# All roots by a product, a place of its own for the fourth weight piece, another word to look at, and finer stages with other dates, in a gated linear recurrence with a SwiGLU block behind it

## The chip, the cores and the metric

The kernel runs on one NeuronCore of one Trainium2 chip. The metric is the device time of one execution in microseconds (us), as a median of several runs. Beside it there is one execution taken by the hardware profiler; all durations of single instructions come from that one. Five engines work side by side, each through its own instructions in the order in which they were written: TensorE (PE, matrix products; its weight loads are listed apart as PEld), VectorE (DVE), ScalarE (ACT), GpSimd (POOL) and SyncE (SP), which here only issues transfers. ACT and POOL issue transfers too. An instruction that waits for another engine or a transfer holds up everything behind it on its own engine.

## The reference

Two blocks follow each other. The first is a recurrence over 768 steps for 4 batches of 8 heads with head size 48. The state of a head is a complex 48 x 48 matrix; its rows decay by a complex gate, and the output is the real part read by q:

```python
mag = np.sqrt(a_re * a_re + a_im * a_im)
scale = np.minimum(mag, 0.999) / (mag + 1e-06)
a_re_n, a_im_n = (a_re * scale, a_im * scale)
for t in range(S):
    new_re = ar * S_re - ai * S_im
    new_im = ar * S_im + ai * S_re
    kv = np.einsum('bhd,bhe->bhde', k[:, :, t], v[:, :, t])
    S_re, S_im = (new_re + kv, new_im)
    y[:, :, t] = np.einsum('bhd,bhde->bhe', q[:, :, t], S_re)
```

Its output, seen as 3072 tokens of 384 features, goes through a feed-forward block:

```python
rms = np.sqrt(np.mean(x * x, axis=-1, keepdims=True) + 1e-06)
xn = x / rms * rms_g
g = xn @ w_gate                        # 384 x 1536
silu = g * (1.0 / (1.0 + np.exp(-g)))
val = xn @ w_val
return (silu * val @ w_out).astype(np.float32)
```

All weights arrive as 64-bit floats, seen as pairs of 32-bit words, and are converted to float32 on the chip.

## The kernel before, in words

**Units and groups.** Each batch's 768 steps are cut into 6 chunks of 128, 24 chunks in all, numbered n. The gates are worked out for "units": chunks 0 and 1 alone, then two chunks at a time (`UNITS`). The feed-forward block takes two chunks at a time (`GROUPS`), 256 tokens.

**Gates** (`gates(u)`, stages "size", "root", "turn", "rot"). Scans over a chunk turn the gates into cumulated magnitudes and phases. ACT supplies squares, roots, arctangent and sines, for which it loads tables, DVE the scans and products. The result, k and q turned by their phase, lies in `rots`, and twelve SP transfers for each pair of chunks (six for each chunk) bring it into the layout by head, `kqs`. The last cumulated values, `ends`, go into `decays`.

**Chunks** (`attend(n)`, line 1135 on). PE computes the scores of k and q for 8 heads in 32-row blocks into banks 4 and 5; DVE copies them under the causal mask into `am` (COPY_PREDICATED). PE then sums `am` times v and q times the old state into bank 6 (`yT`). For the new state PE transposes k into banks 7 and 4, ACT copies it to `kt`, PE multiplies it by v, DVE adds the old state and scales it.

**Norm** (stage "norm"). ACT squares `yT`, PE sums the squares over features by a product with ones into a column of bank 7, DVE scales it into `ssv`, POOL raises it to the power -0.5 into `rs`, one number for each of 128 tokens, one to a partition. It has to be spread over all partitions along the free axis. For the chunks in `SENT` (4 to 21) POOL sends `rs` to a line of `sq` and from there to all partitions of `row`, two transfers one after the other. For the other six chunks PE multiplies `rs`, spread over 128 columns, by the identity into bank 7. DVE multiplies `yg` by the result into `xT`.

**Feed** (`feed(g, xT)`). Six times, PE forms two products of 512 columns (gate and value) in banks 0 to 3, ACT applies SiLU to the one, DVE multiplies the two into `hT`, whose first 3,072 words hold the hidden values of one group. The product with `w_out` follows: plain for groups 0 and 1, and from group 2 on by a scheme with seven instead of eight half-size products.

**Weights** (`narrow(i)`, `fetch`). Twelve pieces: six of 1,536 KB for `w_gate` and `w_val` in turn (512 columns each), then six of 768 KB for `w_out`. Each is brought by a POOL transfer to a place in `wo` or `hT` that is still free, ACT converts its low words in place, and three DVE instructions put the float32 together. After each transfer POOL copies one word of the piece into `junk`: the look that tells POOL that it has landed. Piece i + 2 is sent after the look at piece i. By `CLEAR` the fourth piece (i = 3) also waits until POOL has looked at the `kq` of chunk 1 (`cleared`, copies into `seen`).

**Order.** Nothing is executed as written. `Flow` records every operation with a planned duration, its engine, its data dependences by address range and, for some, a due time. It passes due times back from users to producers, adds a shift for the stage that an operation belongs to (`flow.shift`, keyed by stage name and number), and lays out the program by a list schedule: on each engine, of what is ready, the earliest due time goes first. The instructions are then issued in that order, so the table of shifts and the planned durations decide the order of every engine, SP's and POOL's included, without a change to what is computed. Until a planned time of 62 us, gaps planned for PE are filled with products on `rot` whose result nobody reads, meant as warming (`flow.warm`). All operations are issued at line 676, so the profile tells them apart by tiles.

The last two stores to `out` are issued on SP; then a word `bad` decides by a branch whether a general version runs, which it doesn't with these inputs.

Of the kernel before, what the change touches and what calls it, by code (L numbers as in the profile page):

```python
# [14 lines left out]
ALU = mybir.AluOpType  # L15
# [4 lines left out]
C = 128  # L20
# [441 lines left out]
class Flow:  # L462
# [9 lines left out]
    turn = 0.0  # L472
# [206 lines left out]
def fast(tc, ctx, qT, kT, v, a_re, a_im, w_gate, w_val, w_out, rms_g, out, H, bad):  # L679
# [231 lines left out]

    wwords = wo.rearrange("p c f -> p (c f)").bitcast(I32)
    hwords = hT.bitcast(I32)
    places = [wwords[:, 0:3072], wwords[:, 3072:6144], hwords[:, 3072:6144]] * 2
    raw = wwords[:, 4608:6144]
    places += [raw, hwords[:, 3072:4608], hwords[:, 4608:6144]] * 2

    AHEAD = 2
    landed = {}

    CLEAR = {3: 1}

    def fetch(i, piece, raw, eng):
        to, ap, c, f = piece
        rows, n = to.shape[1:]
        src = ap.bitcast(I32).rearrange("(c p) f -> p c f", p=P)[:, c, 2 * f:2 * (f + n)]
        raw3 = raw.rearrange("p (c f) -> p c f", c=rows)
        if eng == "POOL" and i >= AHEAD:
            wait = [landed[i - AHEAD]]
        elif eng == "POOL":  # L930
            wait = [begun[0]]
        else:
            wait = []
        if eng == "POOL" and i in CLEAR:
            wait = wait + [cleared[CLEAR[i]]]
        dma(raw3, src, eng, after=wait)
        if eng == "POOL":
            landed[i] = copy(junk, raw[0:1, 0:1], eng="POOL")
        words = raw.rearrange("p (n two) -> p n two", two=2)
        return words[:, :, 0], words[:, :, 1]  # L940

# [37 lines left out]
    EARLY = {0: -100.0, 1: -98.0}  # L979
    SUMMED = ()  # L980
    LIGHT = (0, 1, 2)
    SENT = range(4, N - 2)
    SLOW = 2.0
    turn = {}
    moved = {}
# [58 lines left out]
    def gates(u):  # L1044
        ns = UNITS[u]
        nt = len(ns)
        T = nt * C
        t = loaded.pop(u) if u in loaded else load_kq(u, load_gates(u))
        flow.stage = "size", u
        re, im, q, k = (t[x] for x in ("re", "im", "q", "k"))  # L1050
        t1, t2, t3, t4, t5 = (t[f"t{i}"] for i in range(1, 6))
        act(t1, re, AF.Square)
        act(t2, im, AF.Square)
        if u in SUMMED:
            sums = []
            for i in range(nt):
                cs = slice(i * C, (i + 1) * C)
                ps = bank()[:, 0:ND * C].rearrange("p (j t) -> p j t", j=ND)
                mms([(ps, ident, x[:, :, cs], a == 0, a == 1) for a, x in enumerate((t1, t2))],
                    2 * mm_time(ND * C))  # L1060
                sums.append(ps)
                act(t2[:, :, cs], ps, AF.Abs_reciprocal_sqrt)
        else:
            tt(t1, t1, t2, ALU.add)
            act(t2, t1, AF.Abs_reciprocal_sqrt)
        act(t2, t2, AF.Square, scale=-EPS_MAG, bias=ones)
        act(t3, re, AF.Abs_reciprocal_sqrt, due=-200.0 if u == 0 else None)
        act(t3, t3, AF.Square, due=-200.0 if u == 0 else None)
        if u in SUMMED:
            for i in range(nt):  # L1070
                cs = slice(i * C, (i + 1) * C)
                ts(t1[:, :, cs], sums[i], CAP * CAP, None, ALU.min)
        else:
            ts(t1, t1, CAP * CAP, None, ALU.min)
        for j in range(ND):
            for i in range(nt):
                cs = slice(i * C, (i + 1) * C)
                scan(t4[:, j, cs], t2[:, j, cs], t1[:, j, cs], 1.0, ALU.mult, ALU.mult)

        tt(t["f"], t["in"], t3.unsqueeze(1).to_broadcast([P, 2, ND, T]))  # L1080
        stt(im, t5, 2.0, t3, ALU.subtract, rev=True)
        act(re, re, AF.Abs, bias=mid)
        act(re, re, AF.Relu, bias=width, accum=range_[:, u:u + 1])

        flow.stage = "root", u
        root = act(t2, t4, AF.Abs_reciprocal_sqrt)
        act(t1, t2, AF.Square)
        stt(t1, t1, -0.5, t4, ALU.mult)
        stt(t2, t1, 1.5, t2, ALU.add)
        tt(q, q, t4)  # L1090

        roots.append(root)
        yield
        flow.stage = "turn", u
        act(im, im, AF.Arctan, after=roots[-2:])
        last = turn.get(u - 1) if ns[0] % NCH else None
        for j in range(ND):
            scan(t3[:, j], im[:, j], zeros[:, 0:T], last[:, j] if last is not None else 0.0,
                 ALU.add, ALU.add)
        n = t5.bitcast(I32)  # L1100
        act(n, t3, AF.Copy, scale=0.5 / PI)
        stt(im, n, -2 * PI, t3, ALU.mult, ALU.add)
        turn[u] = im[:, :, T - 1:T]
        act(t5, im, AF.Abs)
        act(t3, im, AF.Sin)
        act(t5, t5, AF.Sin, scale=-1.0, bias=halfpi)

        for i, n_ in enumerate(ns):
            e = slice(i * C + C - 1, i * C + C)
            tt(ends[:, :, n_:n_ + 1], t4[:, :, e], t2[:, :, e])  # L1110
        flow.stage = "rot", u
        tt(t["f"], t["f"], t2.unsqueeze(1).to_broadcast([P, 2, ND, T]))
        for i, n_ in enumerate(ns):
            cs = slice(i * C, (i + 1) * C)
            for a, f in enumerate((t5, t3)):
                x = tt(rots[n_ % 2][:, a * ND:(a + 1) * ND].rearrange("p j (o t) -> p j o t", t=C), t["kq"][:, :, :, cs],
                   f[:, :, cs].unsqueeze(2).to_broadcast([P, ND, 2, C]))
                if not started:
                    started.append(x)
        for n_ in ns:  # L1120
            moved[n_] = [dma(kqs[n_ % 2][r:D2:2 * ND], rots[n_ % 2][:, r], "SP") for r in range(2 * ND)]
            if n_ < 2:
                cleared[n_] = copy(seen, kqs[n_ % 2][:, 0, 0:1], eng="POOL")
        send_decays(u)


# [8 lines left out]
    def attend(n):  # L1135
# [12 lines left out]
        for a in range(2):  # L1148
# [3 lines left out]
            for h in range(HH):  # L1152
# [7 lines left out]
            o = am[:, a * HH:(a + 1) * HH]  # L1160
            add("DVE", [(nc.vector.copy_predicated, (), dict(out=pairs(o), mask=mask, data=pairs(s)))],
                0.15 + 1.04e-3 * HH * C, [causal, s, o], [o])
        prev, new = states[(n + 1) % 2], states[n % 2]
        ps = banks[6]
        yT = ps[:, 0:DM].rearrange("p (j t) -> p j t", j=ND)
# [13 lines left out]
                lines[c].append((o, l_, r_, x == 0, x == len(todo) - 1))  # L1179
        order = [lines[c][i] for i in range(len(lines[0])) for c in range(4)]  # L1180
        mms(order, len(order) * mm_time(C) / 4 * 1.06, mode=BLK)
        if not last:
            kt = kts[0]
            for a in range(2):
# [26 lines left out]
        else:  # L1211
# [7 lines left out]
        sv = ssv[:, n:n + 1]  # L1219
        ts(sv, col, 1.0 / DM, EPS_RMS, ALU.mult, ALU.add)  # L1220
        add("POOL", [(nc.gpsimd.tensor_tensor, (), dict(out=rss[n % 2], in0=sv, in1=mhalf,
                                                        op=ALU.pow))], 0.9, [sv, mhalf], [rss[n % 2]])
        if n in SENT:
            line = sq[0:1, 1]
            dma(line, rss[n % 2], "POOL", slow=SLOW)
# [36 lines left out]
    def feed(g, xT):  # L1262
# [28 lines left out]

        def finish():
            for n, ot in zip(ns, ots):
                dma(out[n * C:(n + 1) * C, :], ot)

        if not split:
            for i in range(2):
# [65 lines left out]
    for in_, limit, op in ((ef, P_MIN, ALU.is_ge), (ef, 1.0, ALU.is_le), (range_, 0.0, ALU.is_le),  # L1363
# [15 lines left out]
    flow.warm = dict(after=started, until=WARM, call=[  # L1379
        (nc.tensor.matmul, (banks[3][:, 0:C],), dict(lhsT=filler[:, 0:C], rhs=filler[:, C:2 * C], start=True, stop=True))])  # L1380
    flow.shift = {
        ("attend", 1): 2.2, ("attend", 2): -6.5, ("attend", 4): -25.0, ("attend", 6): -11.5, ("attend", 8): 2.6,
        ("attend", 11): 1.7, ("attend", 12): 1.6, ("attend", 13): 0.9, ("attend", 14): -0.9, ("attend", 16): 1.1,
        ("attend", 17): -2.4, ("attend", 19): -1.4, ("attend", 21): -56.0, ("attend", 22): -0.5,
        ("attend", 23): -2.6, ("feed", 0): 4.7, ("feed", 1): 14.7, ("feed", 3): 31.9, ("feed", 5): 3.0,
        ("feed", 6): 13.5, ("feed", 7): 15.3, ("feed", 8): 7.1, ("feed", 9): 8.2, ("feed", 10): 4.3,
        ("feed", 11): -43.3, ("kq", 0): -8.1, ("kq", 1): 1.6, ("kq", 2): 6.6, ("kq", 3): 54.9, ("kq", 5): -58.9,
        ("kq", 6): 46.3, ("kq", 7): -13.7, ("kq", 9): -3.3, ("kq", 10): 1.9, ("load", 1): 13.9, ("load", 2): -1.6,
        ("load", 3): -5.7, ("load", 9): -5.0, ("norm", 0): -16.0, ("norm", 1): -5.4, ("norm", 2): 0.8,
        ("norm", 3): 2.0, ("norm", 4): -15.2, ("norm", 6): 0.7, ("norm", 9): 0.2, ("norm", 10): 7.3,  # L1390
        ("norm", 11): -1.1, ("norm", 15): -51.1, ("norm", 17): -2.9, ("norm", 19): -11.8, ("norm", 23): -12.0,
        ("root", 0): 1.3, ("root", 1): -4.6, ("root", 2): -43.1, ("root", 3): -3.6, ("root", 4): 0.7,
        ("root", 6): 33.4, ("root", 9): -29.6, ("rot", 0): -25.0, ("rot", 1): 9.8, ("rot", 2): 1.2,
        ("rot", 3): -49.4, ("rot", 5): 0.3, ("rot", 7): 60.9, ("rot", 10): -1.2, ("size", 0): 1.2,
        ("size", 2): -2.8, ("size", 5): 1.5, ("size", 10): -45.3, ("size", 12): -9.1, ("turn", 1): -22.1,
        ("turn", 3): -14.5, ("turn", 8): 38.2, ("turn", 10): 3.3, ("turn", 11): -25.6, ("turn", 12): -4.1,
        ("w", 0): -2.4, ("w", 1): 1.0, ("w", 2): 0.3, ("w", 5): -13.7, ("w", 6): 5.7, ("w", 8): -5.6,
        ("w", 10): 7.1, ("w", 11): 6.2,
    }
    flow.schedule()  # L1400
    with tc.manual_schedule():
# [51 lines left out]
```

## Time and profile before

| what | value |
|---|---|
| median of 5 runs | 727.22 us (723.2 to 730.3) |
| profiled execution, its own time | 726.08 us |
| its span in the trace | 724.4 us |
| PE busy | 683.9 us in 6,900 instructions |
| DVE busy | 475.8 us |
| ACT busy | 327.6 us, 82.1 of it 64 table loads |
| POOL busy | 63.1 us |
| products `ident,rs` | 12 instructions (2 a product), 3.1 us |
| transfers `sq<-rs`, `row<-sq` | 18 each; 2.1 and 3.9 us from issue to landing |
| warming products on `rot` | 82 instructions, 46 of them from 23.8 to 32.0 us |
| first scores of chunk 0 | 32.0 us |
| first product of feed 0 | 55.1 us |
| last product | ends at 717.7 us |

In a line of the profile, `bank<-xT,wg 128*128 128x256 f32` names the written and the read tiles (buffer numbers left out), the part of the array and the shape; a float32 product appears as two instructions. The number after the name is a count or the busy time; what follows an arrow in waits is whom the engine waited for. A stage table gives the busy time of each engine within a stretch of time. The "chain" is followed back from the last instruction through whatever released each step.

### The profile page before, as it was taken

To read this page: it belongs to the slowest core of one execution; us is meant where nothing else is said; L and a number is where in the kernel's file an instruction comes from. 1 tells how busy PE (TensorE), PEld (TensorE's weight loads), DVE (VectorE), ACT (ScalarE), POOL (GpSimd) and SP (SyncE) were. 2 spreads that over 40 slices of the span, in tenths; PEclk is the share of its full clock that TensorE was granted. 3 is DMA by queue.
4 is the path that set the end of the run, shared out by engine and by line. 5 is a ranking of instruction groups with operands and counts; after the bars stand their busy time and mean duration, and the time that the engine had idled before them with its cause. 6 is when DMAs were issued, how large, how long until landed. Compare 5 with 4: busy or idle time off the path is not lost.

```text
span 724.4 us, 16265 instructions
## 1 busy us (share of the span) xinstructions
PE 683.9 (94%) x6900; PEld 601.1 (83%) x6900; DVE 475.8 (66%) x756; ACT 327.6 (45%) x448; POOL 63.1 (9%) x106
## 2 busy tenths in 40 slices
PE   0769989999999999999999999999999999999996
PEld 0768767886889889889889889889889889989995
DVE  8889967987886878778667877778542443125131
ACT  8667547876683664657224753636410120010010
POOL 3141200010001101000011000110100000000000
PEclk9989999999999999999999999999999999999999
DMA  8596674435745463562464733652131231000000
GB/s 298 169 324 172 212 216 98 130 81 143 195 99 155 118 141 70 112 171 87 126 150 125 201 41 106 180 122 84 34 70 29 67 96 22 23 1 2 23 1 27
DMA packets 104001, 81.84 MB, mean 113 GB/s; under 512 B 41936, under 2 KB 94416, under 8 KB 103920
## 3 DMA queue, kind: packets, MB, share of 16 engines
q1 hardware_dynamic: 98704, 64.98, 32.7%
q0 software_dynamic: 4416, 15.35, 9.2%
q8 instruction: 56, 0.92, 0.5%
q10 hardware_dynamic: 800, 0.39, 0.2%
q14 instruction: 25, 0.20, 0.1%
HBM read 55.84 MB, written 4.72 MB: 84 GB/s over the span
## 4 chain that ended last, share of the span: by engine, by line
PE 86%; DVE 7%; DMA 2%; ACT 2%; issue 1%; SPq 1%; POOL 1%; DVEq 0%; ACTq 0%
PE bank L676 86%; DVE wv L676 1%; DVE wo L676 1%; DVE turns L676 1%; DMA decay<-ends 1%; DVE wg L676 1%; SPq L676 1%; DMA in<-in_a_re_dram 1%; DMA kq<-rot 1%; DVE t L676 1%; ACT t L676 1%; POOL rs L676 1%; DVE rot L676 1%; DVE hT L676 0%; DVE am L676 0%
## 5 line engine op out<-in xcount | busy, mean ns | idle before, releaser
L676 PE MATMUL bank<-xT,wg 128*128 128x256 f32 x864 | 202.0, 384 | 0.3 <-DVE xT L676 0.3
L676 PE MATMUL bank<-xT,wv 128*128 128x256 f32 x864 | 199.6, 382 | 1.2 <-DVE hT L676 1.2
L676 PEld LDWEIGHTS bank<-xT,wv 128*128 128x128 f32 x864 | 161.6, 190 | 23.9 <-DVE hT L676 1.6
L676 PEld LDWEIGHTS bank<-xT,wg 128*128 128x128 f32 x864 | 161.8, 191 | 23.2 <-issue 1.0
L676 PE MATMUL bank<-wo,hT 128*128 128x192 f32 (+1 forms) x576 | 118.6, 358 | 0.3 <-DVE hT L676 0.3
L676 DVE TENSOR_TENSOR hT<-bank,sg 128x512 f32<-128x512 f32 x72 | 49.6, 690 | 103.8 <-PE bank L676 96.7
L676 ACT ACTIVATE sg<-bank 128x512 f32<-128x512 f32 x72 | 43.0, 597 | 164.4 <-PE bank L676 158.1
L676 PEld LDWEIGHTS bank<-wo,hT 128*128 128x128 f32 x576 | 96.9, 191 | 12.5 <-issue 1.8
L676 ACT ACT_TABLE_LOAD x64 | 82.1, 1283 | 19.5 <-DVE rot L676 13.3
L676 POOL TENSOR_TENSOR rs<-ssv,mhalf 128x1 f32<-128x1 f32 x24 | 21.9, 914 | 488.6 <-DVE ssv L676 458.2
L676 DVE TENSOR_TENSOR rot<-kin,turns 128x768 f32<-128x768 f32 x48 | 44.1, 952 | 4.4 <-DMA kq<-rot 4.1
L676 PE MATMUL bank<-sums,hT 128*128 128x192 f32 x240 | 44.6, 328 | 0.0
L676 ACT ACTIVATE kt<-bank 128x384 f32<-128x384 f32 x40 | 19.5, 490 | 55.0 <-PE bank L676 52.9
L676 DVE COPY_PREDICATED am<-causal,bank 128x512 f32<-128x512 int32 x48 | 33.5, 724 | 14.6 <-PE bank L676 14.4
L676 ACT ACTIVATE turns<-in 128x768 f32<-128x768 f32 (+1 forms) x39 | 30.0, 789 | 24.6 <-DVE in L676 12.0
L676 PEld LDWEIGHTS bank<-kq 96*32 96x32 f32 x1536 | 30.1, 110 | 12.6 <-issue 7.8
L676 PEld LDWEIGHTS bank<-sums,hT 128*128 128x128 f32 x240 | 39.7, 190 | 0.5
L676 PE MATMUL bank<-kq 96*32 96x32 f32 (+3 forms) x1536 | 35.1, 235 | 4.4 <-issue 1.9
L676 DVE TENSOR_TENSOR hT<-hT 128x768 f32<-128x768 f32 x40 | 38.2, 955 | 0.8
L676 PE MATMUL bank<-am,ve 128*32 128x128 f32 x768 | 37.0, 275 | 0.0
L676 ACT ACTIVATE t<-t 128x768 f32<-128x768 f32 (+1 forms) x39 | 30.8, 789 | 8.8 <-DVE t L676 8.4
L676 PE MATMUL bank<-kq,state 96*32 96x128 f32 x640 | 32.2, 272 | 0.0
(123 smaller groups left out, 726.1 us busy)
## 6 DMA issues: line engine op xcount, KB each, us to landing
kq<-rot SPq DMA_DIRECT2D x144, 128.0 KB, 2.4
kin<-in_q_dram SPq DMA_DIRECT2D x24, 192.0 KB, 4.1
kin<-in_k_dram SPq DMA_DIRECT2D x24, 192.0 KB, 4.1
wo<-in_w_gate_dram SPq DMA_DIRECT2D x6, 768.0 KB, 4.6
out_dram<-ot SPq DMA_DIRECT2D x24, 192.0 KB, 2.3
wo<-in_w_val_dram SPq DMA_DIRECT2D x6, 768.0 KB, 4.6
wo<-in_w_out_dram SPq DMA_DIRECT2D x6, 768.0 KB, 5.0
in<-in_a_re_dram SPq DMA_DIRECT2D x11, 384.0 KB, 4.8
```

The costliest lines, as they stand in the source:

```text
L676: fn(*args, **kw)
```

## The change

- `SENT` is empty: all 24 chunks spread their root by the product.
- `places`: the fourth piece goes to the first half of `hT` instead of the first half of the `wo` room; the fifth and sixth go to the two halves of the `wo` room. The wait for chunk 1's `kq` (`CLEAR`) moves from the fourth to the fifth piece.
- The look reads word 1 of the landed piece, a high word, instead of word 0, a low word that ACT overwrites. It is recorded with the transfer as its only predecessor, and with a planned 0.8 us instead of 0.2.
- The planned duration of the root on POOL goes from 0.9 to 1.2 us, that of the copies into `seen` to 1.2.
- Stage "attend" is cut into "attend", "y" and "state", and the table of shifts is another one.
- The last group's first store (chunk 22) is issued by ACT instead of SP.

```diff
-    places = [wwords[:, 0:3072], wwords[:, 3072:6144], hwords[:, 3072:6144]] * 2
+    places = [wwords[:, 0:3072], wwords[:, 3072:6144], hwords[:, 3072:6144], hwords[:, 0:3072]]
+    places += places[0:2]
...
-    CLEAR = {3: 1}
+    CLEAR = {4: 1}
...
-        dma(raw3, src, eng, after=wait)
+        sent = dma(raw3, src, eng, after=wait)
         if eng == "POOL":
-            landed[i] = copy(junk, raw[0:1, 0:1], eng="POOL")
+            landed[i] = add("POOL", [(nc.gpsimd.tensor_copy, (), dict(out=junk, in_=raw[0:1, 1:2]))], 0.8,
+                            after=[sent])
...
-    SENT = range(4, N - 2)
+    SENT = ()
...
                 cleared[n_] = copy(seen, kqs[n_ % 2][:, 0, 0:1], eng="POOL")
+                cleared[n_]["dur"] = 1.2
...
+        flow.stage = "y", n
         prev, new = states[(n + 1) % 2], states[n % 2]
...
+        flow.stage = "state", n
         if not last:
...
         add("POOL", [(nc.gpsimd.tensor_tensor, (), dict(out=rss[n % 2], in0=sv, in1=mhalf,
-                                                        op=ALU.pow))], 0.9, [sv, mhalf], [rss[n % 2]])
+                                                        op=ALU.pow))], 1.2, [sv, mhalf], [rss[n % 2]])
...
-                dma(out[n * C:(n + 1) * C, :], ot)
+                dma(out[n * C:(n + 1) * C, :], ot, "ACT" if n == N - len(ns) else "SP")
...
     flow.shift = {
-        ("attend", 1): 2.2, ("attend", 2): -6.5, ("attend", 4): -25.0, ("attend", 6): -11.5, ("attend", 8): 2.6,
...
-        ("w", 10): 7.1, ("w", 11): 6.2,
+        ("attend", 0): 29.8, ("attend", 1): -5.3, ("attend", 2): 1.1, ("attend", 3): -21.9, ("attend", 4): -0.4,
...
+        ("kq", 0): 21.0, ("kq", 1): 37.2, ("kq", 2): 93.1,
...
+        ("state", 0): 50.2, ("state", 3): -27.9, ("state", 4): -29.1, ("state", 13): -15.1,
...
     }
```

More of the change, by code (lines that the diff above doesn't have):

```diff
@@ L1381, in fast @@
     flow.shift = {
-        ("attend", 1): 2.2, ("attend", 2): -6.5, ("attend", 4): -25.0, ("attend", 6): -11.5, ("attend", 8): 2.6,
[L1383 to L1396, printed above, removed]
@@ L1397, in fast @@
-        ("w", 0): -2.4, ("w", 1): 1.0, ("w", 2): 0.3, ("w", 5): -13.7, ("w", 6): 5.7, ("w", 8): -5.6,
-        ("w", 10): 7.1, ("w", 11): 6.2,
+        ("attend", 0): 29.8, ("attend", 1): -5.3, ("attend", 2): 1.1, ("attend", 3): -21.9, ("attend", 4): -0.4,
+        ("attend", 5): -4.3, ("attend", 6): -33.5, ("attend", 11): -30.9, ("attend", 16): -9.6,
+        ("attend", 18): -1.0, ("attend", 20): -2.4, ("attend", 22): -3.5, ("attend", 23): -0.6, ("feed", 1): 4.8,
+        ("feed", 4): 5.7, ("feed", 7): 4.3, ("feed", 9): 52.0, ("kq", 0): 21.0, ("kq", 1): 37.2, ("kq", 2): 93.1,
@@ new lines, in fast @@
+        ("kq", 3): -15.0, ("kq", 4): -5.9, ("kq", 7): 1.5, ("kq", 11): 3.9, ("load", 0): 19.0, ("load", 1): -13.9,
+        ("load", 2): -25.3, ("load", 3): 37.3, ("load", 12): 10.4, ("norm", 0): 6.6, ("norm", 2): 0.2,
+        ("norm", 4): 2.3, ("norm", 6): -2.3, ("norm", 11): 4.1, ("norm", 14): -1.1, ("norm", 15): 16.3,
+        ("norm", 19): 5.7, ("norm", 20): 3.5, ("norm", 22): 5.3, ("norm", 23): -13.4, ("root", 0): -11.5,
+        ("root", 1): -6.5, ("root", 2): 0.6, ("root", 3): 17.3, ("root", 4): 2.1, ("root", 9): -11.4,
@@ new lines, in fast @@
+        ("rot", 0): 7.3, ("rot", 1): 5.0, ("rot", 2): -5.1, ("rot", 8): 12.7, ("rot", 9): -17.1,
+        ("rot", 10): -2.9, ("rot", 11): -20.7, ("size", 2): -5.3, ("size", 3): 33.4, ("size", 6): 1.8,
+        ("size", 10): -32.1, ("state", 0): 50.2, ("state", 3): -27.9, ("state", 4): -29.1, ("state", 13): -15.1,
+        ("state", 15): -15.9, ("state", 16): 0.7, ("state", 18): -8.8, ("state", 19): -13.8, ("state", 20): -1.0,
+        ("turn", 0): -2.0, ("turn", 1): 41.3, ("turn", 2): -1.3, ("turn", 3): -47.0, ("turn", 7): 27.7,
@@ L1399, in fast @@
+        ("turn", 8): -11.2, ("turn", 9): 26.8, ("turn", 11): 6.1, ("turn", 12): 6.6, ("w", 0): 10.3,
+        ("w", 2): 0.5, ("w", 3): 0.4, ("w", 5): -2.6, ("w", 7): -11.3, ("w", 10): 0.7, ("w", 11): 17.9,
+        ("y", 1): -4.3, ("y", 5): 2.7, ("y", 8): -13.6, ("y", 9): -6.3, ("y", 13): -1.9, ("y", 15): -6.2,
+        ("y", 18): -3.0, ("y", 19): -1.8,
     }
```

## The prediction

> **What bounds the kernel now.** I read the head of the page first, then the table of busy time by stage, then the chain that ended last, and last the timeline around the instructions that the change touches.
>
> ```profile
> span 724.4 us, 16265 instructions
> ...
> PE 683.9 (94%) x6900; PEld 601.1 (83%) x6900; DVE 475.8 (66%) x756; ACT 327.6 (45%) x448; POOL 63.1 (9%) x106
> ...
> PE 86%; DVE 7%; DMA 2%; ACT 2%; issue 1%; SPq 1%; POOL 1%; DVEq 0%; ACTq 0%
> ```
>
> TensorE (PE) is busy for 94% of the span and makes 86% of the chain. Both are means over two different stages, which the table by stage separates (stage, length, busy time of PE, weight loads, DVE, ACT, POOL, then granted clock, DMA share, GB/s):
>
> ```profile
> 24.00:33.00 9.00, 9.00 (x104) 8.88 (x108) 8.23 (x9) 3.33 (x5) 1.62 (x1) 1.00 0.54 137
> 33.00:45.00 12.00, 9.71 (x207) 9.14 (x195) 10.55 (x11) 7.07 (x12) 4.17 (x4) 0.86 0.88 265
> 45.00:60.00 15.00, 11.17 (x110) 9.31 (x109) 13.63 (x17) 10.60 (x15) 3.58 (x5) 0.89 0.96 313
> 60.00:75.00 15.00, 15.00 (x115) 12.98 (x114) 14.75 (x18) 11.14 (x12) 2.90 (x4) 1.00 0.58 163
> 75.00:90.00 15.00, 13.76 (x61) 11.03 (x60) 14.59 (x22) 8.56 (x11) 4.47 (x6) 1.00 0.61 186
> 90.00:110.00 20.00, 16.33 (x282) 12.25 (x280) 12.45 (x21) 8.94 (x16) 1.56 (x3) 0.91 0.79 222
> ...
> 172.00:250.00 78.00, 78.00 (x875) 67.12 (x865) 63.24 (x101) 47.14 (x63) 4.84 (x8) 1.00 0.55 149
> ```
>
> From 172 us PE has no gap: the chain's last long piece is 540.5 us of PE alone, from 171.6 to 712.1. What is added to PE there moves the end by its whole length; what other engines save there is worth nothing. Before 110 us VectorE (DVE) is nearly full and PE has holes: 2.29 us in 33 to 45, 3.83 in 45 to 60, 1.24 in 75 to 90, 3.67 in 90 to 110, and 0.72 before 172: 11.8 us. Warming products on `rot` between 41 and 55 fill another 6 us (stretches of 1.3, 2.3, 0.9, 0.9, 0.6), and the clock below 1 costs real work some 2.7 us (0.79 from 55 to 60, 0.72 from 97 to 103). So **about 20 us of PE time are lost between 32 and 172 us**, after a start of 32 us.
>
> **The roots: a cost of 4.9 us.** For the 18 chunks 4 to 21 a product of `rs` and the identity replaces two GpSimd DMAs. Six chunks have it already; its price on a full PE is the distance to the next start (start, length, instruction):
>
> ```profile
> 661.64 0.38 PE L676 MATMUL bank<-ident,rs 128*128 128x128 f32 x2
> 661.86 1.14 PE L676 MATMUL bank<-wo,hT 128*128 128x192 f32 x6
> ...
> 665.01 0.39 PE L676 MATMUL bank<-ident,rs 128*128 128x128 f32 x2
> 665.23 0.98 PE L676 MATMUL bank<-hT 128*128 128x192 f32 x5
> ```
>
> 0.22 us here; at 112.77 and 121.56 us, between products of other shapes, it is 0.32. The least is 18 x 0.22 = 4.0 us, the most 18 x 0.38 (the whole length) = 6.8. I take 0.27, between the two kinds of neighbour: 4.9 us, with no cover, for 17 of the 18 lie where PE has no hole. What goes is off the path: 18 x (0.59 + 0.54) = 20 us of POOL, which is 9% busy, and DMAs of 2.1 and 3.9 us, whose wait no PE hole after 172 us shows. The new wait is bank 7, now held until `xT` has read it; behind it stand the next chunk's transposes, then `kt` on ACT. PE has feed products to put there, so I take 0; the upper end is one slow POOL root, 2.1 us, where no feed product is ready.
>
> The Trainium skill ("TensorE: Matmul & The Clock Gate", Back-to-back issue gap) gives about 81 ns for a load and a product of 128 columns in a stream; 36 of them would be an estimated 2.9 us, where the rows give 4.9, and I go by the rows.
>
> **The look at landed weights.** POOL's copy now reads a word that ACT does not overwrite, so ACT need not wait for it:
>
> ```profile
> ACT wo L676 <- POOL junk L676: 4.6, 1, 4.6
> ...
> ACT hT L676 <- POOL junk L676: 1.1, 1, 1.1
> ```
>
> The 4.6 us end at 87.4 us, before a `w_out` piece is converted and before a SiLU at 88.2. PE is full then, and its next hole (94.9 to 96.9) ends with transfers, not with ACT. The end gains between 0 and that 1.8 us hole; I take 0. What is late next is DVE with the same piece.
>
> **The fourth piece.** Its transfer waits today for its place and for chunk 1's `kq`: issued at 37.2 us, looked at by 47.1. In `hT`'s first half the place is free, so it goes once the second piece has been looked at (18.5 us). That moves a 1,536 KB POOL transfer past 12 `kq` transfers of SP (issued 23.8 to 34.9), and lets the fifth and sixth pieces come some 6 us sooner. The first `hT` product (70.3 us) must now wait for the fourth piece's conversion, over at 56.6 today: 0. **The gain** is freedom for DVE. Feed 0 starts at 55.1 because chunk 1's `xT` ends then, and that was late because DVE converted weights first:
>
> ```profile
> 38.18 1.75 DVE L676 CUSTOM_DVE_ANT_0 wv<-wo,wv 128x3072 uint16<-128x3072 uint16 x1
> 41.31 0.56 DVE L676 TENSOR_TENSOR xT<-yg,bank 128x384 f32<-128x384 f32 x1 [1.39 <-PE bank L676]
> 41.78 1.75 DVE L676 SCALAR_TENSOR_TENSOR wg<-hT,wg 128x1536 int32<-128x1536 int32 x1
> 43.56 1.76 DVE L676 CUSTOM_DVE_ANT_0 wg<-hT,wg 128x3072 uint16<-128x3072 uint16 x1
> 45.24 1.32 DVE L676 COPY_PREDICATED am<-causal,bank 128x512 f32<-128x512 int32 x2
> ```
>
> Chunk 1's scores left PE at about 38.1; their mask came at 45.2, 7 us late. **The cost** is contention. Where POOL pieces and `kq` ran together (84 to 98 us, DMA share 0.93 from 90 to 97) `kq` took a median 6.4 us to land; from 20 to 34, where DMA was idle for some 3 us, it took 2.7. So chunk 0's scores, at 32.0 us, may come 0 to 3.7 us later. I take 1, since the piece would be mostly over by 28.
>
> The Trainium skill speaks against this step ("DMA: Bandwidth & Descriptors", Queues, rings and completion order): each DMA engine serves its queue rows in turn, packet by packet, so a large load shares every engine with `kq`. By an equal share, `kq` would take twice 2.7 us, an estimate; the 6.4 us agree in kind.
>
> **Stages, dates and the last store.** The new table moves every engine's order, SP's and POOL's too; no row prices that. It issues no new work, so its bounds are those of the lost time: at best the 20 us come back, and 1.5 us of ACT's first conversion (16.4 to 17.9 us, on the chain); at worst an order adds one more late transfer such as chunk 2's, 5.8 us in the chain at 91 us. The limit in between is DVE: it idles 0.77, 1.45, 1.37, 0.25, 0.41 and 7.55 us in the six early stages, 11.8 together, and its work is the same. I take two thirds, 8 us, nearer to the top, because the mask above and the holes from 90 to 110 are orders rather than work. The last store goes through ACT's queue: an issue took 0.57 to 0.68 us there at the start against 0.33 on SP for the last store, so -0.4 to +0.4; I take 0. The longer planned times of three POOL operations only shift orders.
>
> **Sum.** +4.9 (roots) +1 (contention) -8 (early order) = -2.1. The profiled execution took 726.1 us (724.4 of span and 1.7 around it), 1.1 below the median of 727.2, so about 724 for it, and **725 us** as a median.
>
> **Rivals.** *Packed start, faster* (0.30): the order recovers 14 to 18 of the 20 us, +4.9: -9 to -13, 714 to 718. For: holes of PE beside free DVE from 90 to 110, and 7 us of mask delay. Against: DVE is 98% busy from 60 to 90, and its idle time allows 11.8 us unless warming also shrinks.
> *The piece against `kq`, slower* (0.25): the loads slow both early chunks by 3.7 us or so, and the order gives nothing back; 4.9 + 3.7 and up to 5.8: +8 to +14, 735 to 741. It decides when chunk 0's scores start after 35 us. For: the measured 6.4 us. Against: idle DMA from 22 to 25 us.
> *The order does nothing* (part of the likeliest case): only the roots count, +4.9, 732.
>
> **How the numbers follow.** The likeliest case, 0.45, has early gains of 0 to 10 us and 0 to 1 us of contention, and ends between 722 and 733. A measurement of this kernel can tell about 1% (its runs span 723 to 730), so that case is "within 1%", the packed start is faster, the contention slower. The range, 714 to 738, takes in the packed start but its edge and half of the slow case.
>
> **What will show it.** `ident,rs` instructions up from 12 to 48, no `row` DMA, and PE's time after 172 longer by 4 to 6 us: the roots. `kq` landing over 4 us before 34 us and scores after 34: contention. Feed 0 before 50 us and less than 6 us of holes before 110: packing. ACT waiting for `junk` nowhere: the look. I am wrong if PE has holes after 172 us, from bank 7, or if chunk 2's scores come after 100.

## The result, and the profile after

The changed kernel takes **723.8 us** as a median (721.4 to 727.5), the kernel before 725.7 us in the larger set of runs that this comparison has (its first five gave 727.2). The ratio is 0.9973 with a 95% interval of 0.996 to 0.9986: about 2.0 us less, small, but clear of no change. The profiled execution took 724.2 us, 1.9 below that of before, and its span is 2.0 shorter.

The head of its page, the lines that answer to those shown of before:

```profile
span 722.4 us, 16272 instructions
...
PE 686.1 (95%) x6944; PEld 607.3 (84%) x6944; DVE 475.4 (66%) x756; ACT 340.4 (47%) x457; POOL 43.2 (6%) x70
...
PE 92%; DVE 4%; ACT 1%; issue 1%; DMA 1%; POOL 0%; SPq 0%; DVEq 0%
```

TensorE (PE) has 2.2 us more to do and the span is shorter nevertheless; GpSimd (POOL) has lost the 20 us of transfers. PE now makes 92% of the chain instead of 86%: the part of the start in which VectorE (DVE) was on the chain has shrunk. The same table by stage (stage, length, busy time of PE, weight loads, DVE, ACT, POOL, clock, DMA share, GB/s):

```profile
24.00:33.00 9.00, 9.00 (x65) 9.00 (x64) 8.90 (x10) 5.79 (x6) 0.65 (x1) 1.00 0.82 230
33.00:45.00 12.00, 8.28 (x176) 7.25 (x175) 10.39 (x11) 3.68 (x8) 1.94 (x4) 0.86 0.81 238
45.00:60.00 15.00, 12.37 (x217) 10.60 (x217) 13.68 (x20) 11.72 (x19) 6.64 (x8) 0.85 0.82 246
60.00:75.00 15.00, 15.00 (x66) 13.02 (x65) 14.73 (x17) 10.29 (x12) 4.09 (x5) 0.92 0.68 190
75.00:90.00 15.00, 15.00 (x69) 12.75 (x68) 14.23 (x18) 8.31 (x13) 2.78 (x4) 1.00 0.69 224
90.00:110.00 20.00, 20.00 (x348) 15.09 (x350) 15.20 (x26) 8.99 (x14) 0.56 (x1) 1.00 0.55 147
...
172.00:250.00 78.00, 78.00 (x618) 68.82 (x617) 61.73 (x96) 53.86 (x67) 1.74 (x2) 1.00 0.50 138
```

Two things are to be seen. The holes of PE from 75 to 110 us, 4.9 us before, are gone. And the stage from 33 to 45 is worse than before: 3.7 us of holes instead of 2.3.

A balance by three marks in the two timelines says where the 2 us come from. Feed 0 starts at 58.0 us instead of 55.1: **3.0 lost**. From there to the end of the last product it takes 657.2 us instead of 662.6: **5.3 gained**, although 18 products have been added in that stretch. PE is busy as long there as before (656.7 us, before 656.6); its holes shrink from 5.9 to 0.6 us. From there to the end of the span it is 7.1 instead of 6.8: **0.3 lost**. So the change gained less in the start than PE's holes offered, and not where I had looked for it. The chain fits this: from 58.0 us on it is PE nearly alone, before only from 171.6.

### The profile page after: what moved, and what is told of

Same layout as the page of the kernel before. It is cut to its first block, busy times and chain, and to the rows that moved or that the text cites. A ratio compares the mean times of both kernels' runs of the same rounds, so it can differ in the third digit from the quotient of the medians.

```text
span 722.4 us, 16272 instructions
## 1 busy us (share of the span) xinstructions
PE 686.1 (95%) x6944; PEld 607.3 (84%) x6944; DVE 475.4 (66%) x756; ACT 340.4 (47%) x457; POOL 43.2 (6%) x70
## 4 chain that ended last, share of the span: by engine, by line
PE 92%; DVE 4%; ACT 1%; issue 1%; DMA 1%; POOL 0%; SPq 0%; DVEq 0%
PE bank L676 92%; DVE wv L676 1%; DMA in<-in_a_re_dram 1%; DVE wg L676 1%; DVE t L676 1%; DVE turns L676 1%; DVE rot L676 1%; ACT turns L676 0%; ACT t L676 0%; DVE in L676 0%; DVE am L676 0%; POOL rs L676 0%; ACT L676 0%; DVE hT L676 0%; SPq L676 0%
## 5 line engine op out<-in xcount | busy, mean ns | idle before, releaser
L676 PEld LDWEIGHTS bank<-xT,wg 128*128 128x128 f32 x864 | 163.7, 191 | 22.4 <-DVE xT L676 0.4
L676 PE MATMUL bank<-wo,hT 128*128 128x192 f32 (+1 forms) x576 | 122.9, 359 | 0.4 <-DVE hT L676 0.4
L676 PEld LDWEIGHTS bank<-wo,hT 128*128 128x128 f32 x576 | 95.0, 190 | 13.1 <-issue 1.4
L676 POOL TENSOR_TENSOR rs<-ssv,mhalf 128x1 f32<-128x1 f32 x24 | 24.0, 998 | 523.9 <-DVE ssv L676 519.7
L676 DVE COPY_PREDICATED am<-causal,bank 128x512 f32<-128x512 int32 x48 | 33.1, 724 | 18.5 <-PE bank L676 18.2
L676 ACT ACTIVATE sq<-bank 128x384 f32<-128x384 f32 x24 | 11.8, 490 | 70.4 <-PE bank L676 70.4
L676 PE MATMUL bank<-kq 96*32 96x96 f32 (+3 forms) x1536 | 34.5, 239 | 0.0
```

The source lines that it names most:

```text
L676: fn(*args, **kw)
```

## The experiments

**The price of a product.** Two kernels keep the changed kernel's order, instruction for instruction; one leaves the 18 new products out, one issues each four times.

```diff
     flow.schedule()
+    for x in spread:                     # the 18 products
+        x["calls"] = []                  # no_product;   four_products: x["calls"] * 4
```

> The changed kernel in its own order, with the 18 new root products (chunks 4 to 21) left out and nothing in their place; the output is not the reference's, since those chunks are scaled by what bank 7 held. Theory (PE is full from feed 0 on, a product costs the distance to the next start, 0.22 to 0.32 us): 4.0 to 5.8 us less, taken 4.9, so about 0.993 of the changed kernel. Rival (the price is the wait for the root and for bank 7, not the product): well over 6 us less. Rival (the products lie in gaps that the trace does not show): under 1.5 us less.

Measured: 720.3 us, 3.5 below the changed kernel, 0.19 us a product: a little less than the least that I had expected (4.0), and far from both rivals.

> The changed kernel in its own order, with each of the 18 new products issued four times in a row (the same result each time), so 54 more. Theory: 54 times 0.22 to 0.32 us, 12 to 17 us more, taken 14.6: about 738 us. Rival (the price is the wait, paid once): under 6 us more. Should leaving out and adding give the same price for one product, the price is the product's own.

Measured: 735.6 us, 11.8 above the changed kernel, 0.22 us for each of 54, again just under what I had expected (12 to 17). Taking away and adding agree nearly, so the price is the product's own, not a wait that is paid once. The changed kernel's timeline on PE has the same price as the distance to the next start (start, length, instruction):

```profile
165.78 0.38 PE L676 MATMUL bank<-ident,rs 128*128 128x128 f32 x2
166.00 2.75 PE L676 MATMUL bank<-wo,hT 128*128 128x384 f32 x8
...
172.74 0.38 PE L676 MATMUL bank<-ident,rs 128*128 128x128 f32 x2
172.96 2.75 PE L676 MATMUL bank<-wo,hT 128*128 128x384 f32 x8
```

Of the 18 new products 14 have this distance (0.22 or 0.23 us) and four 0.31 to 0.42, 4.5 us in all. Without the products PE shows 1.1 us of holes between 172 and 700 us, where it has 0.03 with them, which is about what the 3.5 lacks of the 4.5. So the roots are a net cost of 3.5 to 4.0 us.

**The last store.** Both stores on SP, as before.

```diff
-                dma(out[n * C:(n + 1) * C, :], ot, "ACT" if n == N - len(ns) else "SP")
+                dma(out[n * C:(n + 1) * C, :], ot)
```

> The changed kernel with both of the last group's stores on SP again. Read in the trace, from the end of the last DVE instruction to the end of the span: 6.2 us before the change and 6.5 after. Theory (the store's queue matters by some tenths): 6.1 to 6.3 us here. Rival (the store's queue is nothing): 6.5 us again.

Measured: 6.3 us from the last DVE instruction to the end, in one execution. That alone would favour the first theory, but the kernels of the same order with the store on ACT's queue show 6.5 (the change), 6.4 (word zero), 6.2 (no product) and 6.1 (four products), and the other kernels below with the store on ACT's queue 5.3 to 6.5. The queue makes no difference that these traces can tell, and they could not tell one of much less than 1 us.

**The look.** Word 0 instead of word 1, in the same order.

```diff
-            ... dict(out=junk, in_=raw[0:1, 1:2]) ...
+            ... dict(out=junk, in_=raw[0:1, 0:1]) ...
```

> The changed kernel in its own order, with GpSimd looking at word 0 of a landed piece as before the change. Theory (the freed wait was off the path): ACT waits for the look again, some us in all before 110 us, and the time stays within 3 us of the changed kernel. Rival (the look was worth something): 1 us or more longer with PE holes before 110 us.

Measured: 723.8 us, as the changed kernel. In its list of waits before 110 us (engine, what it waited to do, for whom: us, times, longest) the wait is back, longer than any of before:

```profile
ACT hT L676 <- POOL junk L676: 6.2, 1, 6.2
```

It is not on the path: PE has no hole from 58 to 110 us there either. Which word is looked at is worth nothing in this order.

**Scores first.** The timeline of the changed kernel on PE explains a good part of its late start:

```profile
32.80 1.17 PE L676 MATMUL bank<-rot 128*128 128x128 f32 x9
36.39 0.68 PE L676 MATMUL bank<-ot,ot 128*96 128x8 f32 x6 [2.43 <-DVE ot L676]
37.00 1.33 PE L676 MATMUL bank<-kq 96*32 96x128 f32 x64
```

Chunk 0's scores stand behind the small product for chunk 1's decay, which waits for DVE, and behind 36 warming products (23 before). DVE is late because it converts weights first:

```profile
34.49 1.76 DVE L676 CUSTOM_DVE_ANT_0 wg<-wo,wg 128x3072 uint16<-128x3072 uint16 x1
36.16 0.18 DVE L676 TENSOR_TENSOR ot<-ends,ot 128x24 f32<-128x24 f32 x1
```

The landing of `kq` is not what holds the scores here: the five kernels with this order on PE (the change and the four above) have them at 36.1 to 37.3 us, always behind this product, while `kq` landed in a median of 2.6 to 6.1 us. The same-store kernel shows it, with 2.6 us for `kq`, less than before the change:

```profile
36.52 0.68 PE L676 MATMUL bank<-ot,ot 128*96 128x8 f32 x6 [1.77 <-DVE ot L676]
37.13 1.33 PE L676 MATMUL bank<-kq 96*32 96x128 f32 x64
```

The swap:

```diff
     flow.schedule()
+    late = [x for x in flow.ops if x["eng"] == "PE" and x["stage"] == ("rot", 1)][-1]
+    scores = [x for x in flow.ops if x["eng"] == "PE" and x["stage"] == ("attend", 0)]
+    at = max(x["order"] for x in scores[:2])
+    late["order"] = at + 0.25            # and the DVE copy that reads it: at + 0.5
```

> The changed kernel in its own order but for one swap: PE's small product for chunk 1's decay (and the DVE copy that reads it) comes behind the scores of chunk 0 instead of ahead of them. In the changed kernel's trace PE reaches that product at 33.9 us, waits for DVE until 36.4, and the scores follow at 37.0. Theory (DVE's queue sets when feed 0 starts, PE's does not): scores near 34 us, the mask still near 39, feed 0 still at 57 to 59, time within 2 us of 723.8. Rival (the scores' lateness is what moved feed 0 to 58): feed 0 near 55, time 2 to 3 us less.

Measured: 722.3 us (721.0 to 726.5), its ratio to the kernel before 0.9956 (0.9924 to 0.9989), which overlaps the changed kernel's. In the profiled execution, the longest of the nine (726.5 us), the scores are at 33.6 us, yet feed 0 only at 60.5, later than either theory had it. A transfer held it up:

```profile
33.64 1.33 PE L676 MATMUL bank<-kq 96*32 96x128 f32 x64 [1.01 <-DMA kq<-rot]
...
57.58 1.50 PE L676 MATMUL bank<-vn,kt 128*32 128x48 f32 x48 [4.73 <-DMA vn<-in_v_dram]
```

PE waited 4.7 us for `vn`, a small load of SP, and the twelve `kq` transfers from 20 to 36 us took a median of 10.0 us to land. The chain goes through this `vn` (10.0 us) right in front of feed 0, so this execution does not tell whether the late scores moved feed 0 in the changed kernel. Up to the wait it is ahead: chunk 1's `ssv`, from which its root is made, starts at 53.0 us here and at 54.5 there. Whether the swap gains 1 us is open too.

**Undoing one part, with the other parts' dates.** Three kernels change one thing and leave the rest, and the planner lays out the order anew: the fourth to sixth pieces back in the shared places (below), the old stages and dates in the changed kernel, the new stages and dates alone in the kernel before.

```diff
-    places = [wwords[:, 0:3072], wwords[:, 3072:6144], hwords[:, 3072:6144], hwords[:, 0:3072]]
-    places += places[0:2]
+    places = [wwords[:, 0:3072], wwords[:, 3072:6144], hwords[:, 3072:6144]] * 2
...
-    CLEAR = {4: 1}
+    CLEAR = {3: 1}
```

> The changed kernel with the fourth to sixth pieces in the places of before and the wait for chunk 1's transfers on the fourth again; dates of the changed kernel. Theory (the own place lets DVE convert weights while it waits for other work, so PE finds feed 0 and chunk 2 ready): the fourth piece is converted after 45 us, PE gets 5 us or more of holes between 58 and 172 us or starts feed 0 later, time 4 to 12 us more. Rival (the dates alone carry the gain): within 2 us of 723.8. Contention: the transfers of chunk 0 and 1 land in about 2.7 us again instead of 3.4.

> The changed kernel with the stages and the table of dates of before. Theory (the order of the start carries the gain): the holes come back, 5 to 15 us of PE before 172 us, 729 to 739 us. Rival (the place and the look carry it): 723 to 726 us. PE after 172 us stays full under both.

> The kernel before with the stages and the table of dates of the changed kernel and nothing else. Theory (dates fit the parts that they were made for): holes before 172 us grow, 728 to 742 us. Rival (the dates alone are the gain, and the roots a pure cost): 725.7 less 5.6, about 720 us.

Measured: 731.5, 733.3 and 739.3 us; ratios to before 1.0053 (1.0015 to 1.0092), 1.0117 (1.0054 to 1.0179) and 1.0174 (1.0107 to 1.0241). All three lose, as much as their theories said, but only in the first are the holes where the theory put them. With the shared place they come back, by this table of stages in 58 to 110 and 110 to 172 us (5.0 and 3.5 us of PE):

```profile
58.00:110.00 52.00, 47.01 (x423) 37.65 (x422) 48.86 (x69) 34.61 (x46) 9.17 (x13) 1.00 0.77 221
110.00:172.00 62.00, 58.51 (x627) 47.35 (x625) 51.74 (x78) 45.22 (x61) 2.19 (x2) 0.97 0.42 115
```

But feed 0 started at 55.4 there, earlier than in the changed kernel, and `kq` landed in 3.7 us, not in the 2.7 that I had expected back. With the old dates PE has only 0.9 us of holes from 58 to 172 us, and with the new dates alone 4.6, fewer than before (5.6). These two opened holes behind that, 4.2 us (old dates, where I had said that PE stays full) and 9.3 us (new dates alone) from 172 to 690 us. Here is the first:

```profile
172.00:690.00 518.00, 513.85 (x5237) 458.18 (x5236) 316.09 (x517) 210.82 (x282) 13.79 (x18) 1.00 0.33 90
```

So these kernels tell that a table of dates together with parts that it was not made for is 8 to 14 us slower than the kernel that it was made for. They don't tell what the part is worth, because both go together in them.

**Undoing one part, with dates made for it.** Each of the next kernels got its own table, found in the same way: by random steps on the end that the planner foresees. A control does the same to the changed kernel without any other change.

```diff
     flow.shift = {
...
+        (another table of some 170 entries)
     }
```

> The changed kernel with nothing but another table of dates, searched anew by random steps on the planned end; it is the measure for the next two, whose tables are searched in the same way. Theory (dates only reorder a start that DVE limits): 720 to 727 us, PE without holes from feed 0 on. Rival (the changed kernel's dates fit the chip in a way that the planned times don't carry): over 727 us.

Measured: 725.9 us (723.7 to 730.3), 0.9998 of the kernel before (0.9963 to 1.0032), 2.1 us above the changed kernel with the same parts; feed 0 at 56.1, 2.1 us of holes from 58 to 110 and 5.5 from 172 to 690, where I had expected none. So two tables for the same parts can differ by 2 us. How far a search scatters is not measured: each combination of parts below got one table.

> The fourth to sixth pieces in the shared places of before, with the wait on the fourth, and dates searched for these parts. Theory (the own place is worth something by itself): 3 us or more above the control. Rival (the 7.7 us that the shared place cost with the changed kernel's dates were dates that did not fit it): within 2 us of the control.

Measured: **715.0 us** (714.3 to 720.1), 0.9863 of the kernel before (0.9816 to 0.9911), 10.9 below the control and 8.8 below the changed kernel. My theory of the place fell, and so did the rival (within 2 us): with the roots as products and these two tables, giving the fourth piece its own place loses. Where the kernel with the shared place is ahead is read at the start. PE's first scores of chunk 0 are at 29.8 us instead of 37.0, and feed 0 starts here:

```profile
52.54 2.86 PE L676 MATMUL bank<-xT,wg 128*128 128x256 f32 x12 [0.74 <-DVE xT L676]
```

That is 5.5 us earlier than in the changed kernel, and PE then has no hole from 58 to 110 us, 0.04 us to 172, 2.4 us from 172 to 690. PE's clock is higher too. Here is the stage from 58 to 75 us, of this kernel first (columns as in the tables of stages: the clock stands third from the end):

```profile
58.00:75.00 17.00, 17.00 (x80) 14.96 (x80) 16.43 (x15) 9.20 (x13) 4.08 (x6) 1.00 0.70 220
```

then of the changed kernel, and of the same-store kernel, which has its order:

```profile
58.00:75.00 17.00, 16.96 (x71) 14.66 (x72) 16.73 (x23) 12.23 (x15) 4.26 (x6) 0.90 0.70 195
...
58.00:75.00 17.00, 16.50 (x78) 14.48 (x79) 16.11 (x23) 13.00 (x15) 4.03 (x7) 1.00 0.68 200
```

At 0.90 these 17 us do about 1.7 us less work. That the early feed 0 brings the higher clock is not shown: the same-store kernel has 1.00 here with feed 0 at 59.4 us, and the one with the old dates too, with feed 0 at 59.8. The two profiled executions differ by 9.5 us (714.7 and 724.2). 5.5 of them lie in front of feed 0 and 1.1 behind the last product (6.0 us instead of 7.1). In between PE is busy 5.0 us less (651.7 instead of 656.7) and idle 2.1 us more. Of the 5.0 the clock makes some 1.7; the rest is shorter busy time on the same products (`wo` with `hT` alone 118.8 instead of 122.9 us), which have other neighbours in this order; the traces don't divide it into causes. The transfers of chunks 0 and 1 (issues from 20 to 36 us: tiles, queue, count, size, median us to landing) in this kernel:

```profile
kq<-rot SPq DMA_DIRECT2D x12, 128.0 KB, 2.4
```

and in the changed kernel:

```profile
kq<-rot SPq DMA_DIRECT2D x12, 128.0 KB, 3.4
```

What runs beside them differs as well. In the changed kernel POOL sends the fourth piece ahead of the third:

```profile
14.61 0.78 POOL L676 DMA_DIRECT2D hT<-in_w_val_dram  x1
19.15 0.78 POOL L676 DMA_DIRECT2D hT<-in_w_gate_dram  x1 [0.29 <-issue]
```

The third piece then takes 8.8 us to land, beside the first `kq`. With the shared place and its own dates the third goes at 14.8 us, much as before the change (14.4), has landed by 23, and no further piece is sent until 37.1.

> The roots of chunks 4 to 21 sent by two transfers as before, all else as in the changed kernel, with dates searched for these parts. Theory (the product is a pure cost of 0.19 to 0.22 us on a full PE, and the transfers are hidden once the order allows for them): 3.5 to 4 us below the control, near 720 us, PE full after 172 us. Rival (the transfers' 6 us and more from root to use open holes after 172 us): at the control or above, holes of several us after 172 us.

Measured: 722.1 us (718.6 to 726.2), 0.9941 of the kernel before (0.9911 to 0.9970), 3.7 below the control. The size is the one that leaving out the products gave, but it lies not far above the 2 us by which two tables for the same parts differed, and PE has 6.9 us of holes from 172 to 690, where the theory had it full. So it agrees with the price of the product and is not a second proof.

> The shared places of before for the fourth to sixth pieces and the roots of chunks 4 to 21 sent by transfers, the look, stages and last store of the changed kernel, dates searched for these parts. Theory (both undone parts are costs of the change, the product 3.5 to 4 us and the early transfer the rest, and they add): 3 to 4 us below the 715.0 of the shared place alone, 711 to 712 us, feed 0 near 52.5 us, first scores near 30. Rival (the transfers of the roots need slack that this order lacks): 715 us or more, holes of PE after 172 us above the 2.4 us of the shared place alone.

Measured: 719.3 us (713.0 to 720.9, and one run of 1,436.6 that the ratio leaves out; the median without it is 719.0), 0.9903 of the kernel before (0.9856 to 0.9949). The two gains did not add up: it is not 3 to 4 us below the shared place alone. Whether it is above it, by 4.3 us of the medians, is not clear, since the two intervals overlap. With the roots sent by transfers the shared place is thus worth 2.8 us (722.1 and 719.3, intervals that overlap), not 10.9. Either the two parts bear on each other, or the tables of one search scatter by several us; one table for each can't tell. Holes after 172 us are not the reason, 1.8 us from 172 to 690 in the profiled execution. In the trace feed 0 starts at 55.7 us, 3.2 later, behind a mask for which PE waited 3.2 us. This execution took 714.4 us and was one of the two shortest; where the others lose 4 to 6 us more, no trace here shows.

All kernels side by side: median, chunk 0's first scores and the start of feed 0 on PE in the profiled execution (us).

| kernel | median | first scores | feed 0 |
|---|---|---|---|
| before | 725.7 | 32.0 | 55.1 |
| the change | 723.8 | 37.0 | 58.0 |
| scores first | 722.3 | 33.6 | 60.5 |
| shared place, the change's dates | 731.5 | 31.5 | 55.4 |
| old dates | 733.3 | 34.6 | 59.8 |
| new dates alone | 739.3 | 31.6 | 57.0 |
| control, own dates | 725.9 | 37.7 | 56.1 |
| shared place, own dates | 715.0 | 29.8 | 52.5 |
| without the products, own dates | 722.1 | 35.5 | 56.1 |
| both, own dates | 719.3 | 32.8 | 55.7 |

In these executions the first scores are at 32.8 us or earlier in every kernel with the shared place and later in every other. Feed 0 before 55 us was seen once, with the shared place, the products and their own dates.

## Why the prediction was right or wrong

The forecast of 725 us, and of about 2 us less than before, came true; "within 1%" as well. Its terms did so less well. The roots cost about 1 us less than I had said and the rest gained about 1 us less, so that the sum came out so near is luck. Of the signs that I had named, 48 instructions `ident,rs`, no `row` transfer, no wait of ACT for `junk`, no holes after 172 us and chunk 2's scores before 100 us (at 93.6) were there; `kq` landing over 4 us and feed 0 before 50 us were not.

**The roots, 4.9 us.** The mechanism held: PE is full, every product moves the end. The size was off: 3.5 to 4.0 us. I had taken 0.27 us as a middle between two kinds of neighbour; 14 of the 18 new products have 0.22 or 0.23, all together a mean of 0.25, and without them 1.1 us of holes opened. The bound at the lower end, 4.0, would have been the better value. The estimate of 2.9 us by the Trainium skill ("TensorE: Matmul & The Clock Gate", Back-to-back issue gap) lay below what was measured. Bank 7, which I put at 0, shows no PE hole after 172 us: right.

**The contention, 1 us.** The weakest step. The change of the landing times is there: `kq` landed in a median of 3.4 us in the changed kernel's profile against 2.7 before, and in 2.6, 3.9, 5.8, 6.1 and 10.0 us in the five variants that keep its early order but for a detail. But it did not set what I had tied to it. The mark that I had named, chunk 0's scores after 35 us, was reached, at 37.0, for another reason: PE's own queue, with the decay product that waits for DVE, held the scores there with 2.6 us of landing as with 6.1. Three executions of this order (same store, the change, word zero) with 2.6, 3.4 and 3.9 us took 723.7, 724.2 and 724.0 us. And where the swap took the product away, PE did wait for `kq`, 1.0 us at a median of 10.0; its longest wait before feed 0 was the one for `vn`, 4.7 us.

I also had the transfers in the wrong order. I expected the fourth piece after the look at 18.5 us, and the fifth and sixth some 6 us sooner. In the changed kernel the fourth went at 14.6 us and the third at 19.2; the sixth went 15.2 us sooner (32.4) and the fifth 7.0 later (47.5). What the own place costs in all, its loads, their order on POOL and the order of DVE and PE that it leads to, was 10.9 us in one pair of fitted kernels and 2.8 in the other, less what one search differs from another, of which only one case is known (2.1 us). Which of these makes it up stays open. I had that rival at 3.7 us.

The Trainium skill ("DMA: Bandwidth & Descriptors", Queues, rings and completion order) says that a DMA engine takes turns between queue rows packet by packet, and it spoke against this step. The traces agree in direction: 2.4 to 2.7 us without a weight load beside `kq`, 2.6 to 10.0 with one. By an equal share 2.4 would become an estimated 4.8.

**The early order, 8 us gained.** Near in size, wrong in place. I expected the gain in front of feed 0, through the late mask of chunk 1, and gave feed 0 before 50 us as the mark. Feed 0 came 3.0 us later instead: chunk 1's mask did follow its scores closely now (from 47.2 us, the scores from 45.8), but the scores themselves were 9 us later than before. The gain lies behind it: 4.9 us of holes from 75 to 110 and 0.6 from 110 to 172 are gone. The 5.3 us net, with 3.5 to 4.0 for the products put back, make 8.8 to 9.3 gained from feed 0 on; less the 3.0 at the start, some 6 remain, against my 8 less 1. The holes account for 5.5; the rest is not split further, and the runs don't tell the place's share from that of the dates. The limit by DVE's idle time (11.8 us) held for this kernel, but it is none in general: the shared place with its own dates, 10.7 us below before although it pays for the products, gained some 14.

**The look and the last store, 0 each**: right for the word that is looked at; the store's worth is too small for these traces.

**The rivals.** "Packed start" did not happen in this change, but its time was reachable: 715.0 us is inside its 714 to 718, with the change's roots and look, and with the old place of the fourth piece, though with feed 0 at 52.5 us, not before 50. Of "the piece against `kq`" the sign came true without its cause.

## What to carry to other kernels

A part of a change that comes with a newly made order can't be priced by undoing it under that order: here undoing the place cost 7.7 us, and once each side had an order of its own it gained 10.9 in one pair of kernels and 2.8 in the other. Make the order anew for both sides and for the unchanged kernel too, and more than once for each: the one control here moved by 2.1 us, which is one draw and no bound. Where one engine is full, an added instruction costs its distance to the next start among the neighbours that it will really have, and leaving it out wins less where holes open in its place. A sign that a theory names, such as late scores, is worth little until the trace shows what they waited for.

## What the runs showed of the hardware that I had not expected

The landing time of the same twelve `kq` transfers varies widely between executions of nearly the same order. In the three kernels whose POOL sent no weight piece between 15 and 37 us (before, the shared place with its own dates, and both) the median was 2.4 to 2.7 us. In the eleven others, which sent one piece of 1,536 KB at 18 to 21 us and another at 31 to 34, it was 2.6 to 10.0. In the execution with 10.0 us these two loads took 11.0 and 11.6 us, and a `vn` transfer was late enough to stop PE for 4.7 us. Dates that count on one landing time may therefore fit one execution and miss the next.
